# A second MLP's rows transposed two to three steps further down, and one slot's last products taken by halves

## The chip, the cores and the metric

The kernel runs on one core of a Trainium2 chip. The metric is the device time of one execution in microseconds. Besides, one execution was recorded by the hardware profiler; all rows below come from it. Engines: PE is TensorE, DVE is VectorE, ACT is ScalarE, POOL is GpSimd, SP is the engine that mostly issues DMAs (its queue is SPq, that of ScalarE ACTq).

## The reference

Three stages run one after the other.

```python
# 1 attention of 2 x 8 heads, 768 rows, head size 64; a pair counts only if both fall in one hash bucket
scores = np.where(q_bucket[:, :, :, None] == k_bucket[:, :, None, :], scale * q @ k.T, -1e9)
x = softmax(scores) @ v                               # -> 1536 tokens x 512
# 2 a mixture of 8 experts, one per token (512 -> 1024 -> 512)
e_idx = argmax(x @ w_gate + modality_bias[modality_id])
x2[e_idx == e] = gate_w * (relu(x[e_idx == e] @ w1[e]) @ w2[e])
# 3 a second, dense MLP (512 -> 2048 -> 512) on all 1536 tokens
h = x2 @ w_in
out = (maximum(h, 0) + log1p(exp(-abs(h)))) @ w_out
```

All is in float32. A product of the experts or of the MLP is made of three: each operand is split in a high and a low part, and high x high, high x low and low x high are summed.

## The kernel before, in words

**Experts.** The tokens are sorted by expert into slots of 128. Slots 0 to 16 always run; four more stand under a branch that this input doesn't take. `pipe` writes the slots out as a pipeline: the first layer of slot s (`g1`, four chunks c), its `relu`, its transposes (`hT`), and between them the second layer of slot s-1 (`g2`). `split` turns one raw weight chunk into its high part (ACT, L995) and its low part (DVE, L1000). `yout` scales a slot's result and scatters its rows with an indirect DMA (POOL, L1128) into `x2_dram`, in sorted order, with the token's number in column 513. The profile prints `x2_dram` as `x_dram`, and the tile `x2` of the second MLP as `x`.

**Second MLP.** The sorted rows are 12 tiles j of 128, in three groups g of four tiles. `x2load(j)` loads a tile into one of two buffers (`x2_p`, `bufs=2`). `x2prep(j)` transposes it on PE (`ps_x`, four 128x128 transposes, L1252), makes the high part on ACT (`x2H`, L1254) and the low part on DVE (`x2L`, L1255), and copies column 513 to `oidx` (L1258, on DVE for j = 4 and 5, else on POOL). Tile j+2 goes into the buffer of tile j, so its load waits until all readers of tile j are done, the copy to `oidx` included.

`mlp()` runs steps n over `seq`, in which four blocks f of 128 hidden units are taken for g = 0, then for g = 1, then for g = 2. Step n issues `mlp1(g, f)` (12 products into `ps_f`, three ACT passes `ga`, on DVE `gg`, then `gH` and `gL`) and then `mlp2` of the step before (12 products into `ps_o`). In steps 1, 2, 5 and 9 the DVE also converts a weight block (`wconv`, three passes that make `w` from the loaded `wraw`), and `wsplit` makes `mwH` (ACT) and `mwL` (DVE) of a block converted before. `wload` loads the next block on SP's queue. Step 0's `mlp1` is issued earlier, among the experts.

Each engine works through its own instructions in the order in which this code issues them. Group 1 is first used in step 4, group 2 in step 8. Loads of tiles 0 to 3 are issued by ACT, those of 4 to 11 by SP.

Of the kernel before, what the change touches and what calls it, by code (L numbers as in the profile page):

```python
# [16 lines left out]
P = 128  # L17
# [462 lines left out]
class Moe:  # L480
# [651 lines left out]
    def pipe(self, a, b, hook):  # L1132

        if a > 1:
            self.order(a, b)
            for _ in range(3):
                self.split()
            self.xT(a)
        for s in range(a, b + 1):
            if a + 2 <= s + 2 < b and s > 1:  # L1140
                self.gather(s + 2)
            if s < b:
                for c in range(4):
                    self.g1(s, c)

                    if s > a or c != 2:
                        self.split()
                    elif s + 1 < b:
                        self.xT(s + 1)
                self.relu(s)  # L1150
                self.reload()
            hook(s, 0)
            for c in range(4):
                if s > a:
                    self.g2(s - 1, c)
                    self.split()
                if s < b and c in (1, 2):
                    self.hT(s, c - 1)
                    if s == a and c == 2:
                        self.split()  # L1160
                if a < s < b - 1 and c == 0:
                    self.xT(s + 1)
            self.reload()
            hook(s, 1)
            if s > a:
                self.yout(s - 1)
# [68 lines left out]
    def x2load(self, j):  # L1235
        t = self.x2_p.tile([P, self.D + 1], F32, tag="x2", name="x2")

        r = (j + 2) % self.TT * P
        (self.nc.scalar if j < 4 else self.nc.sync).dma_start(out=t, in_=self.x2_dram[r:r + P, :])
        self.x2[j] = t  # L1240

    def x2prep(self, j):
# [108 lines left out]
    def mlp(self):  # L1351

        NF, CH, pend = self.NF, self.CH, self.pend
        NG = self.TT // 4
        seq = [(g, c * CH + k) for c in range(NF // CH) for g in range(NG) for k in range(CH)]
        self.late.update(seq[-CH:])

        for f in range(CH, NF):
            c, k = divmod(f, CH)
            at = (c - 1) * NG * CH + (1, 2, 5, 9)[k]  # L1360
            conv, then = self.step.get(seq[at], ((), []))
            self.step[seq[at]] = (f, then + [(self.wsplit, CH - 1)] * (f == CH))
            self.step[seq[at + 1]] = ((), [(self.wsplit, f)] + [(self.wload, f + 2)] * (f + 2 < NF))
        for n, (g, f) in enumerate(seq):

            j = 4 + 2 * {0: 0, 2: 1, 3: 2, 5: 3}.get(n, NF)
            if j < self.TT:
                if n:
                    self.x2prep(j - 2)
                    self.x2prep(j - 1)  # L1370
                self.x2load(j)
                self.x2load(j + 1)
            elif n == 6:
                self.x2prep(self.TT - 2)
                self.x2prep(self.TT - 1)
            if n == len(seq) - CH:
                self.sA.close()
                self.x2b = self.sA.enter_context(self.tc.tile_pool(name="late", bufs=1, reuse_waits="tile"))
            if n:
                pend.append((g, f) + self.mlp1(g, f))  # L1380
            if len(pend) > 1 and pend[0][:2] not in self.late:
                self.mlp2(*pend.pop(0))

        last = [(i, x) for i in range(4) for x in pend]
        n = len(pend)
        last[n - 1:n + 1] = last[n:n + 1] + last[n - 1:n]
        for i, x in last:
            self.mlp2(*x, tiles=[i])
# [245 lines left out]
```

## Time and profile before

| | |
|---|---|
| time, median of 3 runs | 771.82 us (771.51 to 772.5) |
| the profiled execution: time | 769.36 us |
| the profiled execution: span from first to last instruction | 767.6 us |
| PE busy | 748.5 us, 98% of the span |
| DVE, ACT, POOL busy | 596.5, 522.3, 227.9 us |
| mean granted clock of TensorE | 0.996 |

A busy PE means that a product was in flight; the products of the MLP follow each other every 0.23 us though each lasts 0.39 us. Idle time of another engine costs nothing by itself.

### The profile page before, as it was taken

The page shows a single profiled execution, that of the slowest core. Times are in us where ns is not written, and L with a number is a line of the kernel's source. Part 1 is how long each engine was busy: PE and PEld are TensorE (multiplying, and loading weights), DVE is VectorE, ACT ScalarE, POOL GpSimd, SP SyncE. Part 2 cuts the span into 40 slices and gives each one's busy share as a digit, 9 for nine tenths or more (in the row PEclk, how much of TensorE's full clock was granted, in tenths as well). Part 3 has the DMA queues.
Part 4 walks back from the last instruction along what each step waited for, and adds up shares of the span by engine and source line. Part 5 has one row for each costly group of instructions (what it writes and reads, how often), then busy time and mean ns, then how long its engine had stood idle before and what let it go on. Part 6 is the DMA issues. An engine that isn't in the chain of part 4 may idle for free.

```text
span 767.6 us, 13126 instructions
## 1 busy us (share of the span) xinstructions
PE 748.5 (98%) x4232; PEld 646.6 (84%) x4232; DVE 596.5 (78%) x894; ACT 522.3 (68%) x872; POOL 227.9 (30%) x608
## 2 busy tenths in 40 slices
PE   8999999999999999999999999899999999999995
PEld 6899999999999867888888888688888888888874
DVE  6898888989888889999999999765557557564442
ACT  5787887877879758899898999464544344433330
POOL 4554544446565567322312132200000000000222
PEclk9999999999999999999999999999999999999999
DMA  8845637536480014679973642351111113000111
GB/s 197 192 122 132 166 73 165 149 93 166 144 243 30 2 49 133 219 242 358 362 269 116 206 153 83 101 183 65 56 54 59 53 55 110 1 0 1 55 56 55
DMA packets 72602, 95.29 MB, mean 124 GB/s; under 512 B 31842, under 2 KB 48226, under 8 KB 72528
## 3 DMA queue, kind: packets, MB, share of 16 engines
q1 hardware_dynamic: 67152, 83.85, 36.6%
q0 software_dynamic: 3744, 9.45, 3.5%
q10 hardware_dynamic: 1632, 1.08, 0.5%
q8 instruction: 35, 0.57, 0.3%
q14 instruction: 39, 0.32, 0.1%
HBM read 105.18 MB, written 10.76 MB: 151 GB/s over the span
## 4 chain that ended last, share of the span: by engine, by line
PE 91%; POOL 2%; DVE 2%; issue 2%; DMA 1%; ACT 1%; POOLq 0%; ACTq 0%; SPq 0%; DVEq 0%
PE ps_f L1302 17%; PE ps_o L1335 17%; PE ps_y L1116 11%; PE ps_g L1069 10%; PE ps_o L310 9%; PE s L253 9%; PE ps_t L286 8%; PE s L332 2%; PE ps_prep L184 2%; PE ps_ht L1087 2%; PE ps_prep L178 2%; PE ps_xt L1042 1%; PE ps_x L1252 1%; DMA x<-x_dram 1%; POOL xg L987 1%
## 5 line engine op out<-in xcount | busy, mean ns | idle before, releaser
L1000 DVE TENSOR_TENSOR wL<-wr,wH 128x1024 fp32r<-128x1024 f32 (+1 forms) x137 | 161.3, 1207 | 9.0 <-ACT wH L995 8.9
L995 ACT CAST wH<-wr 128x1024 fp32r<-128x1024 f32 (+1 forms) x144 | 141.4, 1005 | 8.7 <-PE ps_g L1069 3.6
L1304 ACT ACTIVATE ga<-ps_f 128x512 f32<-128x512 f32 x48 | 28.7, 599 | 128.8 <-PE ps_f L1302 125.2
L263 DVE TENSOR_REDUCE mx<-s 128x1 f32<-128x768 f32 x96 | 91.5, 954 | 20.7 <-PE s L332 17.3
L274 ACT ACTIVATE p<-s,nb,sc 128x768 f32<-128x768 f32 x96 | 95.9, 999 | 15.9 <-POOL nb L265 13.1
L1310 DVE SCALAR_TENSOR_TENSOR gg<-ps_f,ga 128x512 f32<-128x512 f32 x48 | 33.2, 692 | 94.0 <-ACT ga L1306 92.0
L296 DVE TENSOR_TENSOR PL<-ps_t,PH 128x512 fp32r<-128x512 f32 x144 | 98.3, 683 | 6.8 <-ACT PH L291 6.4
L291 ACT CAST PH<-ps_t 128x512 fp32r<-128x512 f32 x144 | 83.7, 587 | 15.1 <-PE ps_t L286 12.6
L253 PE MATMUL s<-K,Q 76*128 76x384 f32 (+1 forms) x384 | 88.4, 351 | 2.6 <-ACT K L239 0.9
L310 PE MATMUL ps_o<-PH,vhl 128*128 128x256 f32 x288 | 86.8, 317 | 0.4 <-ACT Os L316 0.4
L286 PE MATMUL ps_t<-ident,p 128*128 128x128 f32 x576 | 86.3, 272 | 0.6 <-DVE PL L296 0.6
L1344 POOL DMA_INDIRECT out_dram<-acc,oidx x12 | 11.7, 972 | 231.0 <-DVE acc L1342 227.9
L1302 PE MATMUL ps_f<-x2H,mwH 128*128 128x512 f32 x192 | 76.1, 396 | 0.7 <-PEq L1206 0.7
L1335 PE MATMUL ps_o<-mwH,gH 128*128 128x512 f32 x192 | 75.5, 393 | 0.4 <-DVE gH L1317 0.4
L1335 PE MATMUL ps_o<-mwL,gH 128*128 128x512 f32 x192 | 75.8, 395 | 0.0
L1302 PE MATMUL ps_f<-x2H,mwL 128*128 128x512 f32 x192 | 75.6, 394 | 0.0
L1302 PE MATMUL ps_f<-x2L,mwH 128*128 128x512 f32 x192 | 75.6, 394 | 0.0
L1335 PE MATMUL ps_o<-mwH,gL 128*128 128x512 f32 x192 | 75.6, 394 | 0.0
L286 PEld LDWEIGHTS ps_t<-ident,p 128*128 128x128 f32 x576 | 69.4, 141 | 2.5 <-PE s L253 0.9
L310 PE MATMUL ps_o<-PL,vhl 128*64 128x256 f32 x288 | 68.3, 280 | 0.0
L253 PEld LDWEIGHTS s<-K,Q 76*128 76x128 f32 (+1 forms) x384 | 63.2, 189 | 4.3 <-ACT p L274 1.7
L1128 POOL DMA_INDIRECT x_dram<-y,cpi x17 | 19.0, 1118 | 125.9 <-ACT y L1123 89.6
(293 smaller groups left out, 1654.5 us busy)
## 6 DMA issues: line engine op xcount, KB each, us to landing
wr<-in_moe_w_dram SPq DMA_DIRECT2D x136, 512.0 KB
wraw<-in_moe_w_in_dram SPq DMA_DIRECT2D x16, 512.0 KB
wraw<-in_moe_w_out_dram SPq DMA_DIRECT2D x16, 512.0 KB
Q<-qH SPq DMA_DIRECT2D x28, 192.0 KB
K<-kH SPq DMA_DIRECT2D x28, 192.0 KB
rawv<-in_v_dram SPq DMA_DIRECT2D x8, 384.0 KB
x_dram<-x SPq DMA_DIRECT2D x8, 384.0 KB
rawq<-in_q_dram SPq DMA_DIRECT2D x14, 192.0 KB
```

What stands on the lines that cost most here:

```text
L253: self.nc.tensor.matmul(s[:, h, :HS], d[l, j][:kk, ts], d[r, j][:kk, h * HS:(h + 1) * HS], start=(a == 0), stop=(a == 1))
L263: nc.vector.tensor_reduce(mx, s[:, :, :self.HS], axis=AX.XY, op=ALU.max)
L274: self.nc.scalar.activation(e["P"][ti].rearrange("p (h c) -> p h c", h=2), s[:, :, :self.HS], AF.Exp, scale=sc, bias=nb, accum_out=e["sum" ...
L286: self.nc.tensor.transpose(ps[:, kk, t], e["P"][t][:, kt * P:(kt + 1) * P], self.ident)
L291: self.nc.scalar.copy(e["PH"][:, 2 * bk:2 * bk + 2].rearrange("p k n -> p (k n)"), e["T", bk])
L296: self.nc.vector.tensor_tensor(e["PL"][:, sl].rearrange("p k n -> p (k n)"), e["T", bk], e["PH"][:, sl].rearrange("p k n -> p (k n)").bitc ...
L310: self.nc.tensor.matmul(O[:n, :2 * P], vh[:, j, kt, :n], e[nm][:, kt], start=(kt == 0 and n == P), stop=(kt == NT - 1 and n == P))
L995: self.nc.scalar.copy(self.wt[s, c][0][:, sl], self.raw[c][:, sl])
L1000: eng.tensor_tensor(L[:, sl], self.raw[c][:, sl], H[:, sl].bitcast(F32), op=ALU.subtract)
L1116: nc.tensor.matmul(ps, a[:, f], ww[:, w], start=(f == 0 and n == 0), stop=(f == self.KF - 1 and n == 2))
L1302: nc.tensor.matmul(ps, w[:, 0, sl], x[:, k], start=(k == 0 and n == 0), stop=(k == self.KD - 1 and n == 2))
L1335: nc.tensor.matmul(self.ops[i], a[:, sl], w[:, 1], start=(k == 0 and n == 0), stop=(k == self.CH - 1 and n == 2))
```

## The change

Three edits.

1. In `mlp()` the calls of `x2prep` and `x2load` move. Tiles 4 and 5 are transposed ahead of `mlp1` of step 3 (before: step 2), tiles 6 and 7 behind `mlp1` of step 3 (before: ahead of it), tiles 8 and 9 behind `mlp1` of step 5 (before: ahead of it), tiles 10 and 11 behind `mlp1` of step 7 (before: ahead of that of step 6). The loads of tiles 6 to 11 move along, each pair behind the transposes that free its buffers.
2. The loads of tiles 4 to 7 are issued by ACT instead of SP.
3. In the slot that a pipeline starts with (slot 1), the last chunk's six products are ordered by halves of the output: three for the first 512 columns, then three for the second.

```diff
             if s < b:
                 for c in range(4):
-                    self.g1(s, c)
+
+                    self.g1(s, c, (0, 1) if s == a and c == 3 else None)
...
-        (self.nc.scalar if j < 4 else self.nc.sync).dma_start(out=t, in_=self.x2_dram[r:r + P, :])
+        (self.nc.scalar if j < 8 else self.nc.sync).dma_start(out=t, in_=self.x2_dram[r:r + P, :])
...
+        def rows(js):
+            for x, j in zip((self.x2prep, self.x2load), js or ()):
+                if j:
+                    x(j)
+                    x(j + 1)
         for n, (g, f) in enumerate(seq):
 
-            j = 4 + 2 * {0: 0, 2: 1, 3: 2, 5: 3}.get(n, NF)
-            if j < self.TT:
-                if n:
-                    self.x2prep(j - 2)
-                    self.x2prep(j - 1)
-                self.x2load(j)
-                self.x2load(j + 1)
-            elif n == 6:
-                self.x2prep(self.TT - 2)
-                self.x2prep(self.TT - 1)
+            rows({0: (None, 4), 3: (4, 6)}.get(n))
...
             if n:
                 pend.append((g, f) + self.mlp1(g, f))
+            rows({3: (6, 8), 5: (8, 10), 7: (10, None)}.get(n))
             if len(pend) > 1 and pend[0][:2] not in self.late:
                 self.mlp2(*pend.pop(0))
```

On VectorE, from the low part of weight block 3 (`mwL_8081`) on, before (tile 4 is `x_8049`, tile 5 `x_8051`; `mwL_8151` is block 4):

```order
L1291 TENSOR_TENSOR mwL_8081<-w_8030,mwH_8080 128x1024
L1255 TENSOR_TENSOR x2L<-ps_x_8102,x2H 128x4x128
L1258 CAST oidx<-x_8049 128x1
L1255 TENSOR_TENSOR x2L<-ps_x_8111,x2H 128x4x128
L1258 CAST oidx<-x_8051 128x1
L1310 SCALAR_TENSOR_TENSOR gg<-ps_f,ga 128x512
L1276 TENSOR_SCALAR w_8145<-wraw 128x1024
L1319 TENSOR_TENSOR gL<-gg,gH 128x512
L1278 SCALAR_TENSOR_TENSOR w_8145<-wraw,w_8145 128x1024
L1280 SCALAR_TENSOR_TENSOR w_8145<-wraw,w_8145 128x1024
L1291 TENSOR_TENSOR mwL_8151<-w_8075,mwH_8150 128x1024
```

And the same stretch of VectorE now:

```order
L1292 TENSOR_TENSOR mwL_8081<-w_8030,mwH_8080 128x1024
L1311 SCALAR_TENSOR_TENSOR gg<-ps_f,ga 128x512
L1277 TENSOR_SCALAR w_8122<-wraw 128x1024
L1320 TENSOR_TENSOR gL<-gg,gH 128x512
L1279 SCALAR_TENSOR_TENSOR w_8122<-wraw,w_8122 128x1024
L1281 SCALAR_TENSOR_TENSOR w_8122<-wraw,w_8122 128x1024
L1292 TENSOR_TENSOR mwL_8128<-w_8075,mwH_8127 128x1024
L1256 TENSOR_TENSOR x2L<-ps_x_8148,x2H 128x4x128
L1259 CAST oidx<-x_8049 128x1
L1256 TENSOR_TENSOR x2L<-ps_x_8157,x2H 128x4x128
L1259 CAST oidx<-x_8051 128x1
```

The work on tiles 4 and 5 went behind all of step 2's DVE work. On ScalarE, from the end of the experts (the branch) on, the rows before are these (`mwH_8080` is block 3):

```order
L1206 UNCONDITIONAL_BRANCH x2
L1304 ACTIVATE ga<-ps_f 128x512
L1305 ACTIVATE ga<-ga 128x512
L1306 ACTIVATE ga<-ga 128x512
L1315 CAST gH<-gg 128x512
L1290 CAST mwH_8080<-w_8030 128x1024
```

Now two DMA issues, the loads of tiles 4 and 5, stand ahead of step 1's passes:

```order
L1207 UNCONDITIONAL_BRANCH x2
L1240 DMA x_8049<-x_dram 128x513
L1240 DMA x_8051<-x_dram 128x513
L1305 ACTIVATE ga<-ps_f 128x512
L1306 ACTIVATE ga<-ga 128x512
L1307 ACTIVATE ga<-ga 128x512
```

The loads came from SP's queue, where nothing but weight loads stood behind them. On PE the transposes of tiles 6 and 7 (`x_8165`, `x_8167`) now stand between the first-layer products of step 3 and the second-layer products of step 2:

```order
L1303 MATMUL ps_f<-x2H,mwL_8081 128x512
L1253 MATMUL ps_x_8199<-ident,x_8165 128x128 x4
L1253 MATMUL ps_x_8207<-ident,x_8167 128x128 x4
L1336 MATMUL ps_o<-mwH_7425,gH 128x512
```

Everything that PE issues behind them is the same as before, but for the pairs 8 and 9 and 10 and 11, which moved in the same way.

## Rows read from the trace of the kernel before

**Rows 1.** The waits, PE: line, releaser, us in total, times, longest.
```profile
PE ps_x L1252 <- DMA x<-x_dram: 2.9, 1, 2.9
...
PE ps_ht L1087 <- ACT h L1077: 0.9, 1, 0.9
```

**Rows 2.** The chain that ended last, 484 to 500: start, length, what.
```profile
488.73 3.40 DMA x_dram<-y,cpi
...
492.20 4.21 DMA x<-x_dram
```

**Rows 3.** The timeline, PE, second MLP: start, length, then the instruction.
```profile
493.21 0.39 PE L1335 MATMUL ps_o<-mwH,gL 128*128 128x512 f32 x1
...
503.15 1.03 PE L1252 MATMUL ps_x<-ident,x 128*128 128x128 f32 x8
503.94 0.48 PE L1302 MATMUL ps_f<-x2H,mwH 128*128 128x512 f32 x1
...
506.82 0.39 PE L1335 MATMUL ps_o<-mwH,gH 128*128 128x512 f32 x1
...
509.77 0.40 PE L1302 MATMUL ps_f<-x2L,mwH 128*128 128x512 f32 x1
...
533.82 0.40 PE L1302 MATMUL ps_f<-x2L,mwH 128*128 128x512 f32 x1
```

**Rows 4.** The timeline, SP's queue, second MLP.
```profile
490.12 0.39 SPq L1265 DMA_DIRECT2D wraw<-in_moe_w_in_dram  x1
...
492.20 0.82 SPq L1239 DMA_DIRECT2D x<-x_dram  x2
...
499.86 0.32 SPq L1239 DMA_DIRECT2D x<-x_dram  x1
...
503.82 0.85 SPq L1239 DMA_DIRECT2D x<-x_dram  x2
```

**Rows 5.** The timeline, ACT, second MLP.
```profile
490.91 0.60 ACT L1304 ACTIVATE ga<-ps_f 128x512 f32<-128x512 f32 x1 [2.93 <-PE ps_f L1302]
```

**Rows 6.** The timeline, DVE, second MLP.
```profile
492.87 0.69 DVE L1310 SCALAR_TENSOR_TENSOR gg<-ps_f,ga 128x512 f32<-128x512 f32 x1 [2.78 <-ACT ga L1306]
...
498.39 0.68 DVE L1255 TENSOR_TENSOR x2L<-ps_x,x2H 128x512 fp32r<-128x512 f32 x1
...
502.54 0.69 DVE L1310 SCALAR_TENSOR_TENSOR gg<-ps_f,ga 128x512 f32<-128x512 f32 x1 [2.75 <-ACT ga L1306]
...
508.06 1.28 DVE L1255 TENSOR_TENSOR x2L<-ps_x,x2H 128x512 fp32r<-128x512 f32 x2
509.26 0.68 DVE L1310 SCALAR_TENSOR_TENSOR gg<-ps_f,ga 128x512 f32<-128x512 f32 x1
...
511.57 1.22 DVE L1291 TENSOR_TENSOR mwL<-w,mwH 128x1024 fp32r<-128x1024 f32 x1 [0.26 <-ACT mwH L1290]
...
534.30 0.69 DVE L1319 TENSOR_TENSOR gL<-gg,gH 128x512 fp32r<-128x512 f32 x1
```

**Rows 7.** The timeline, POOL, second MLP.
```profile
502.66 0.18 POOL L1258 CAST oidx<-x 128x1 int32<-128x1 f32 x1 [0.61 <-DMA x<-x_dram]
...
510.39 0.18 POOL L1258 CAST oidx<-x 128x1 int32<-128x1 f32 x1 [0.50 <-DMA x<-x_dram]
```

**Rows 8.** Busy times by stretch: length, engines, then PE's granted clock, DMA share, GB/s.
```profile
10.00:12.00 2.00, 0.64 (x2) 0.19 (x1) 1.91 (x5) 1.24 (x3) 1.84 (x5) 1.00 0.98 212
14.00:16.00 2.00, 2.00 (x11) 2.00 (x10) 1.87 (x4) 1.06 (x3) 1.25 (x5) 0.50 1.05 269
16.00:18.00 2.00, 2.00 (x10) 2.00 (x9) 1.04 (x3) 2.00 (x4) 1.15 (x3) 0.69 0.78 203
494.00:496.00 2.00, 0.00 (x0) 0.00 (x0) 1.91 (x3) 1.16 (x2) 0.00 (x0) 1.00 0.97 360
```

**Rows 9.** The timeline, ACT, the end of slot 1's first layer.
```profile
287.86 1.05 ACT L995 CAST wH<-wr 128x1024 fp32r<-128x1024 f32 x1
288.81 1.09 ACT L1077 ACTIVATE h<-ps_g 128x512 f32<-128x512 f32 x2
```

## The prediction

> **What bounds the kernel now.** I read the waits of PE first. PE is the engine on which the chain of waits ends nearly everywhere, so only its idle time can be won, and only new idle time on it can be lost. Two of its waits lie where the change works: 2.9 us for the load of tile 4, and 0.9 us for slot 1's `h` [rows 1]. Then the chain around the first: the last slot's scatter lands at 492.13, SP issues the loads of tiles 4 and 5 at 492.20, tile 4 is there 4.21 us later [rows 2], while PE has issued its last product of `mlp2(0)` at 493.21 [rows 3]. Then the timeline of each engine behind that, because the change moves work on all of them. The reader is to see there that PE runs without a gap from 496.55 on, and that DVE is nearly as full: step 1's work takes it from 492.87 to 498.39, step 2's from 502.54 to 508.06, 5.52 us each [rows 6], with no idle time shown inside either.
>
> All starts are in the profiled execution, 769.36 us long, which is 2.46 us under the median; I add the difference to the median of 771.82.
>
> **The removed wait.** Without the transposes of tiles 4 and 5 in step 2, PE goes on at 493.45 (493.21 plus the pitch of 0.23) with `mlp1` of step 2, which needs only group 0. By itself that is worth up to 2.9 us. The question is what is late next.
>
> **ACT is held at the scatter.** The two load issues now stand on ACT ahead of step 1's `ga`. They need the landing at 492.13, just as SP's did, so they go out at 492.20 and take 0.82 us [rows 4]. ACT is free at 493.02 instead of starting `ga` at 490.91 [rows 5]. From `ga` to `gg` it is 492.87 - 490.91 = 1.96 us [rows 5, 6], so `gg` of step 1 starts at 494.98, 2.11 later. No row of before shows an ACT issue that waits, so the bounds are 0 (ACT passes it by) and 2.1 us (ACT stands). I take 2.1, because ACT's instructions start in program order wherever I looked in the timeline. The Trainium skill speaks against this edit too: "TensorE: Matmul & The Clock Gate", section on the 16 sub-arrays, says that ScalarE and VectorE take their queue strictly first in, first out, and only PE reorders a little. By that the forecast stands as given below; if a waiting issue were passed by, the time would be some 2.1 us less.
>
> **Tiles 6 and 7 come late: the main term.** Their loads go into the buffers of 4 and 5 and cannot go out before `oidx` of 4 and 5 has been copied on DVE. In the order now, that copy stands behind all DVE work of steps 1 and 2. Step 2's work is ready when DVE comes to it: ACT is through with `gH` and `mwH` at most 2.31 us behind a `gg` (509.26 to 511.57, where `mwL` had to wait for `mwH`), and `ga` takes 1.96 more, which makes 499.3, while DVE is through with step 1 at 500.5 [rows 6]. So the low part of tile 4 starts 2 x 5.52 = 11.04 us behind `gg`, at 506.02 [rows 6]. In the trace of before, tile 7's load went out at 499.86, 1.47 us after tile 4's low part had started at 498.39 [rows 4, 6]. Now that is 507.49, issued by ACT, which holds step 3's `ga` meanwhile.
>
> How long that load takes: 2.80 us when hardly anything else moved (499.86 to 502.66), 6.1 at the other end (the second issue of the pair at 503.82, some 0.49 later, to 510.39) [rows 4, 7]. I take 4.3. The nearest case is tile 4's own load, which took 4.21 with a weight block issued 2.08 us ahead of it [rows 2, 4]. Here the load of block 7 goes out on SP as soon as DVE has converted block 5, about 1.8 us ahead of tile 6's load. So tile 7 is there at 511.8, its transposes start 0.14 later, as tile 4's did, and take half of 0.79 us [rows 3]; `mlp2` of step 2 starts at 512.3.
>
> PE stands before these transposes from about 503.1. Up to that point it has 2.8 us for `mlp1(2)`, 0.4 waiting for step 1's late `gH` and `gL`, 2.8 for `mlp2(1)`, 0.8 for the transposes of 4 and 5, 2.9 for `mlp1(3)`, counted from 493.45. It then stands idle for some 8 us. Before, `mlp2` of step 2 started at 506.82 with exactly the same work behind it [rows 3]. The loss here, with the removed wait already counted in, is 512.3 - 506.8 = **5.5 us**.
>
> With the load's other values it is 4.0 and 7.3. The lower end is cut off by a second chain. ACT is free at 507.9, `gg` of step 3 follows at 509.9, `mwL` of block 5 2.31 us later, then 1.22 for it and 1.28 for the low parts of tiles 6 and 7 [rows 6]: 514.7. The second product of step 4 needs these and stood at 509.77 [rows 3]. So the range is 4.9 to 7.3.
>
> **Tiles 10 and 11 come late for step 8.** They are now transposed behind `mlp1` of step 7, with only `mlp2` of step 6 between them and their first use. Their low parts stand on DVE behind `gL` of step 7. That `gL` started at 534.30; it comes 0.79 earlier against the rest, since the pair's transposes no longer stand ahead of it. So the low parts are done at 534.30 - 0.79 + 0.69 + 1.28 = 535.5 [rows 3, 6], and the second product of step 8, which needs all of them, stood at 533.82 [rows 3]: **1.6 us** of new waiting (1.0 to 1.7). PE is without gaps behind it, so nothing gives it back. Tiles 8 and 9 have a whole step more and cost nothing.
>
> **The clock.** After the long idle time PE's granted clock may fall. In the trace it was at 0.50, that is 1.2 of 2.4 GHz, over all of 14 to 16 us and still 0.69 on average from 16 to 18, shortly after a stretch in which PE was busy for 0.64 of 2 us; after the 2.9 us of waiting at 493.6 it stayed at 1.00 [rows 8]. An idle time of 8 us is far over both, so I expect a fall. About 3.3 us at half speed (2 from the one stretch, 1.24 from the other) lose **1.7 us**. The ends are 0, as after 493.6, and 3.4, if it stays low twice as long. The Trainium skill, same page, section on what is actually happening, holds the slow state to be the normal one, which activity lifts; the trace agrees, and by it the 1.7 belong in the sum; without them it would come out at 779.
>
> **Slot 1 by halves.** The aim must be the 0.9 us in front of `hT` [rows 1]. But ACT starts `relu` at 288.81, without idle time, straight behind a weight cast that began at 287.86 [rows 9]. The first half could be ready earlier and ACT would still not take it. I take 0; the bounds are -0.9, the whole wait, and +0.2, should the low weight part be late for the second product.
>
> **Sum:** 5.5 + 1.6 + 1.7 + 0 = 8.8 us. 769.36 + 8.8 = 778.2 for the profiled execution, 771.82 + 8.8 = **780.6 us** for the median.
>
> **Rivals.**
> - *The clock stays up* after the idle time: 771.8 + 7.1 = 778.9. The 2.9 us at 493.6 speak for it, the fall at 14 us against. Chance 0.15.
> - *ACT is not held at the scatter:* all of the DVE chain comes 2.1 earlier, and with it tile 7: 780.6 - 2.1 = 778.5. Against it, the order of ACT. Chance 0.1.
> - *The loads of 6 and 7 take about 6 us* beside the weight block: 780.6 + 1.8 = 782.4. Chance 0.1.
> - *Not slower:* tile 7 is loaded behind `mlp1(3)`, because its issue waits only for the transposes of 4 and 5 and not for DVE. PE then runs through from 493.45 and `mlp2` of step 2 starts at 503.9, 2.9 us early; less the 1.6 at step 8, 770.5. It decides from where load 7 goes out: by 500.3, it is there when PE is done at 503.1 (with 2.80 us). For it: before, tile 7 was there at 502.66, half a microsecond ahead of its use [rows 3, 7]. Against it: SP's issue at 499.86 came only after tile 4's low part at 498.39 and what follows it on DVE, long after the transposes of 496.55. Chance 0.05.
> - The forecast itself: 0.6.
>
> **Numbers.** A difference under 0.2%, 1.5 us, can't be told from no change. The not slower case lies just within it or a little under, so faster 0.02, same 0.04, slower 0.94. For the range I take the lower rivals together at the bottom, ACT not held and the clock up, 771.8 + 5.0 = 776.8, and a little below; at the top slow loads with a somewhat longer low clock, 783.5. 776.5 to 783.5 leaves about 0.15 outside.
>
> **What would show it.** In the trace of the changed kernel: `ga` of step 1 starts some 2 us later on ACT, behind two ACTq issues at about 492.2; DVE works from `gg` of step 1 to `oidx` of tile 5 without a gap; PE waits some 8 us for the load of tile 6 or 7 with all of `mlp1(3)` behind it; the granted clock is 0.50 in a stretch right there; the second product of step 8 waits 1.6 us for `x2L`; and the wait for `h` in slot 1 is still about 0.9. If the two loads go out before DVE has reached tile 4, the main term is wrong; if PE's wait there is under 3 us, the sign may be.

## The result: 7.5 us slower

Over four runs each, the changed kernel takes a median of 779.21 us (778.27 to 779.97) and the kernel before 771.66 (771.13 to 772.5). The ratio is 1.0102, with an interval of 1.0086 to 1.0118. The profiled execution of the changed kernel took 779.03 us, with a span of 777.3. (The transposes moved by half a step to one and a half steps, as the list of the change has it, and not by two to three, as the title says.)

Before any start time is compared, one shift has to be taken out. ACT's last `y` of the MoE starts at 488.39 in this execution, and 487.29 in the profiled execution of before; the scatter behind it lands 1.10 us later. Other executions with the same code up to there have it at 487.34 or 488.44, so this is no work of the change. In this section, differences that hang on the scatter are less 1.10.

PE's waits over the whole span (line, releaser, us in total, times, longest):

```profile
PE ps_x L1253 <- DMA x<-x_dram: 8.1, 1, 8.1
PE ps_f L1303 <- DVE x2L L1256: 1.4, 1, 1.4
...
PE ps_ht L1087 <- ACT h L1077: 0.8, 1, 0.8
```

The 2.9 us for tile 4 [rows 1] are gone. In their place stand 8.1 us for tile 6 and 1.4 us for low parts in step 8. Slot 1's wait for `h` is as it was. The next three views show how the 8.1 come about. First ACT's timeline in the second MLP (start, length, instruction, idle time before it and what ended it):

```profile
488.39 0.69 ACT L1123 ACTIVATE y<-ps_y,gsl 128x512 f32<-128x512 f32 x1 [2.67 <-issue]
493.25 0.81 ACTq L1240 DMA_DIRECT2D x<-x_dram  x2
494.11 0.60 ACT L1305 ACTIVATE ga<-ps_f 128x512 f32<-128x512 f32 x1 [5.04 <-DMA x_dram<-y,cpi]
...
507.88 0.98 ACTq L1240 DMA_DIRECT2D x<-x_dram  x2
508.91 0.60 ACT L1305 ACTIVATE ga<-ps_f 128x512 f32<-128x512 f32 x1 [4.06 <-DVE oidx L1259]
```

Twice a `ga` stands right behind two DMA issues and is released by what the *issue* waited for: once by the landing of the scatter, once by `oidx` on DVE. `ga` of step 1 moved from 490.91 [rows 5] to 494.11, which is 2.1 us less the shift. DVE's timeline has what follows from it:

```profile
496.07 0.69 DVE L1311 SCALAR_TENSOR_TENSOR gg<-ps_f,ga 128x512 f32<-128x512 f32 x1 [4.89 <-ACT ga L1307]
...
501.59 0.69 DVE L1311 SCALAR_TENSOR_TENSOR gg<-ps_f,ga 128x512 f32<-128x512 f32 x1
...
504.82 1.23 DVE L1281 SCALAR_TENSOR_TENSOR w<-wraw,w 128x1024 int32<-128x1024 int32 x1
505.96 1.22 DVE L1292 TENSOR_TENSOR mwL<-w,mwH 128x1024 fp32r<-128x1024 f32 x1
507.10 0.68 DVE L1256 TENSOR_TENSOR x2L<-ps_x,x2H 128x512 fp32r<-128x512 f32 x1
507.70 0.14 DVE L1259 CAST oidx<-x 128x1 int32<-128x1 f32 x1
```

From the first `gg` to tile 4's low part it is 11.03 us, without an idle time between. The last three rows show who is served in which order: a conversion and a split of a weight block, then tile 4's low part, then the copy for which the load of tile 6 waits. The load itself takes 4.52 us (the chain that ended last: start, length, what):

```profile
507.88 4.52 DMA x<-x_dram
```

PE's timeline around it, and in step 8:

```profile
500.62 1.04 PE L1253 MATMUL ps_x<-ident,x 128*128 128x128 f32 x8
...
504.06 0.40 PE L1303 MATMUL ps_f<-x2H,mwL 128*128 128x512 f32 x1
512.53 1.94 PE L1253 MATMUL ps_x<-ident,x 128*128 128x128 f32 x8 [8.08 <-DMA x<-x_dram]
514.12 0.78 PE L1336 MATMUL ps_o<-mwH,gH 128*128 128x512 f32 x1
...
517.79 0.40 PE L1303 MATMUL ps_f<-x2L,mwH 128*128 128x512 f32 x1
...
543.38 0.50 PE L1303 MATMUL ps_f<-x2L,mwH 128*128 128x512 f32 x1 [1.41 <-DVE x2L L1256]
```

`mlp2` of step 2 starts at 514.12, against 506.82 [rows 3]: 6.2 us later. The products of `mlp2` themselves take no longer: 0.39 to 0.40 us each from 515.49 on, as before. Those at 512.53 and 514.12 are, and the busy times by stretch say why (length, PE, PEld, DVE, ACT, POOL, PE's granted clock, DMA share, GB/s):

```profile
506.00:508.00 2.00, 0.00 (x0) 0.00 (x0) 2.00 (x5) 0.00 (x0) 0.00 (x0) 1.00 0.33 46
508.00:510.00 2.00, 0.00 (x0) 0.00 (x0) 0.50 (x2) 1.06 (x2) 0.00 (x0) 0.64 1.00 360
...
512.00:514.00 2.00, 1.47 (x7) 1.50 (x8) 1.51 (x2) 1.49 (x3) 0.70 (x2) 0.50 0.06 21
514.00:516.00 2.00, 2.00 (x9) 1.68 (x8) 1.70 (x3) 0.83 (x2) 0.00 (x0) 0.66 0.62 158
```

The clock fell to 0.50 (1.2 GHz) at about 508.6, in the middle of the idle time, and came back at about 515.4. PE had work only from 512.53 on, so 2.8 us of work ran at half speed and lost 1.4.

### The profile page after: what moved, and what is told of

It reads as the page before. It is cut to its first block, busy times and chain, and to the rows that moved or that the text cites. A ratio compares the mean times of both kernels' runs of the same rounds, so it can differ in the third digit from the quotient of the medians.

```text
span 777.3 us, 13129 instructions
## 1 busy us (share of the span) xinstructions
PE 751.1 (97%) x4231; PEld 647.3 (83%) x4232; DVE 596.4 (77%) x894; ACT 522.0 (67%) x872; POOL 232.8 (30%) x608
## 4 chain that ended last, share of the span: by engine, by line
PE 88%; DVE 3%; POOL 2%; issue 2%; DMA 2%; ACT 1%; POOLq 0%; ACTq 0%; DVEq 0%
PE ps_f L1303 16%; PE ps_o L1336 16%; PE ps_y L1116 11%; PE ps_g L1069 10%; PE ps_o L310 9%; PE s L253 8%; PE ps_t L286 8%; PE s L332 2%; PE ps_prep L184 2%; PE ps_ht L1087 2%; PE ps_prep L178 1%; PE ps_xt L1042 1%; PE ps_x L1253 1%; DMA x<-x_dram 1%; POOL xg L987 0%
## 5 line engine op out<-in xcount | busy, mean ns | idle before, releaser
L1128 POOL DMA_INDIRECT x_dram<-y,cpi x17 | 22.3, 1312 | 123.2 <-ACT y L1123 88.9
```

## The experiments

All were timed against runs of the kernel before on the same chip. "+" and "-" are against that median.

**What the two loads on ACT cost.** The changed kernel, with the loads of tiles 4 to 7 back on SP.

```
-        (self.nc.scalar if j < 8 else self.nc.sync).dma_start(out=t, in_=self.x2_dram[r:r + P, :])
+        (self.nc.scalar if j < 4 else self.nc.sync).dma_start(out=t, in_=self.x2_dram[r:r + P, :])
```

> The changed kernel with the loads of tiles 4 to 7 back on SP's queue. Theory (ACT stands at the scatter and holds all of VectorE's work behind it): step 1's ga starts 2 us earlier, tile 7's load goes out about 2 us earlier and, with no weight block just ahead of it, takes about 3 us; some 3 us faster than the changed kernel, about +4.7 us against before (+3.3 if the clock stays up). Rival (which engine issues the loads doesn't matter, the copy of oidx alone decides): within 0.5 us of the changed kernel.

Measured: 775.19, +3.8, ratio 1.0048 [1.0031, 1.0064]. `ga` of step 1 is free of the scatter. The loads of 6 and 7 leave 3.4 us earlier, of which 0.9 is the scatter's earlier landing in this execution, and tile 6 is there 2.76 us after its issue, with no weight block just ahead of it. PE still waits for tile 6:

```profile
490.60 0.60 ACT L1305 ACTIVATE ga<-ps_f 128x512 f32<-128x512 f32 x1 [2.41 <-PE ps_f L1303]
```
```profile
504.44 0.98 SPq L1240 DMA_DIRECT2D x<-x_dram  x2
```
```profile
507.34 1.94 PE L1253 MATMUL ps_x<-ident,x 128*128 128x128 f32 x8 [4.80 <-DMA x<-x_dram]
```

So by the medians some 3.8 of the 7.5 us are due to the choice of ACT. The trace shows that the saving was larger and that the clock took part of it back. It fell at about 506.4 and came back at about 513.2, with PE at work for nearly all of that time:

```profile
506.00:508.00 2.00, 0.66 (x3) 0.69 (x4) 1.44 (x2) 1.22 (x2) 0.74 (x1) 0.59 0.91 294
508.00:510.00 2.00, 2.00 (x9) 1.79 (x9) 1.23 (x3) 1.17 (x2) 0.64 (x2) 0.50 0.99 311
510.00:512.00 2.00, 2.00 (x6) 1.58 (x5) 0.62 (x1) 0.00 (x0) 0.00 (x0) 0.50 0.98 344
512.00:514.00 2.00, 2.00 (x8) 1.57 (x7) 0.00 (x0) 0.00 (x0) 0.18 (x1) 0.70 0.13 49
```

That lost 2.8 us, twice as much as in the changed kernel; the table near the end has it beside the others.

**What the copy on DVE costs.** The changed kernel, with `oidx` of tiles 4 and 5 copied on POOL, as of all others.

```
-        (nc.vector if g == 1 and i < 2 else nc.gpsimd).tensor_copy(self.oidx[g][:, i:i + 1], x[:, self.D:])
+        nc.gpsimd.tensor_copy(self.oidx[g][:, i:i + 1], x[:, self.D:])
```

> The changed kernel with the oidx copies of tiles 4 and 5 on GpSimd instead of VectorE, loads still on ACT. Theory (the loads of tiles 6 and 7 wait for that copy behind two steps of VectorE work): the loads go out behind the high parts on ACT, some 3.5 us earlier; PE's wait for them falls from 8.1 to about 3.5 to 4 us; then VectorE's low parts of tiles 6 and 7 bind, which leaves about +3.8 us against before. Rival (the load itself or the transfers beside it make the wait): the wait stays over 7 us and the time within 1 us of the changed kernel.

Measured: 773.8, +2.4 where +3.8 was expected, ratio 1.0034 [1.0021, 1.0048]. The loads left at 501.50 instead of 507.88, and still PE waited:

```profile
501.50 0.81 ACTq L1240 DMA_DIRECT2D x<-x_dram  x2
```
```profile
506.20 1.28 DVE L1256 TENSOR_TENSOR x2L<-ps_x,x2H 128x512 fp32r<-128x512 f32 x2
```
```profile
506.94 1.25 PE L1253 MATMUL ps_x<-ident,x 128*128 128x128 f32 x8 [3.38 <-DVE x2L L1256]
```

This releaser was in no account so far: the expectation had the low parts of tiles 6 and 7 as the next bound, and this is that of tile 4. Transposes go to one of two PSUM buffers, and tile 6 needs the one that tile 4's low part on DVE still reads; that low part started at 506.20. So a load that comes in time would not have been enough. DVE holds PE back in two ways, the copy and the PSUM buffer, and the first one is only the longer. The clock fell behind this wait too (0.58 and 0.57 in 508 to 512), which cost 1.6 us.

**What tiles 8 to 11 cost.** The changed kernel, with their transposes back ahead of steps 5 and 6.

```
-            rows({0: (None, 4), 3: (4, 6)}.get(n))
+            rows({0: (None, 4), 3: (4, 6), 5: (8, 10), 6: (10, None)}.get(n))
...
-            rows({3: (6, 8), 5: (8, 10), 7: (10, None)}.get(n))
+            rows({3: (6, 8)}.get(n))
```

> The changed kernel with tiles 8 to 11 back where they were (ahead of steps 5 and 6). Theory: the 1.4 us that PE waits for low parts in step 8 is gone and nothing else changes, so 1.4 us faster than the changed kernel, about +6.1 against before. Rival (that wait is slack which a later one takes up): the same time as the changed kernel.

Measured: 777.19, +5.8, ratio 1.008 [1.0057, 1.0103]. The wait in step 8 is gone, the one for tile 6 stays at 7.9 us. The time is some 1.8 us less than the changed kernel's. That fits the wait in step 8, which put back the products behind it by 1.7 us: step 8's first product starts 7.99 us later than before, those behind the wait 9.66.

**What the halves in slot 1 do.** The kernel before, with this edit alone.

```
-                    self.g1(s, c)
+                    self.g1(s, c, (0, 1) if s == a and c == 3 else None)
```

> The kernel before with the third edit alone (slot 1's last products by halves). Theory (ACT takes the relu only behind its weight cast, so an earlier half wins nothing): 0 us against before, within 0.3, and PE still waits 0.8 to 0.9 us for h in slot 1. Rival (the wait for h is the products' order): 0.9 us faster, and that wait gone.

Measured: 771.21, -0.2, ratio 1.0 [0.9985, 1.0015]. The `relu` still starts straight behind a weight cast on ACT, and PE waits 0.9 us for it, as before [rows 1, 9]:

```profile
288.61 1.05 ACT L995 CAST wH<-wr 128x1024 fp32r<-128x1024 f32 x1
289.56 1.09 ACT L1077 ACTIVATE h<-ps_g 128x512 f32<-128x512 f32 x2
```

**The loads of 4 to 7 on ACT alone**, in the kernel before.

```
-        (self.nc.scalar if j < 4 else self.nc.sync).dma_start(out=t, in_=self.x2_dram[r:r + P, :])
+        (self.nc.scalar if j < 8 else self.nc.sync).dma_start(out=t, in_=self.x2_dram[r:r + P, :])
```

> The kernel before with the second edit alone: loads of tiles 4 to 7 on ACT. Theory (ACT stands at the scatter and then at the copy of oidx): step 1's gg starts 2.1 us later, all of VectorE's work behind it too, tile 7's load goes out 2.1 us later beside a weight block, and PE, which had that load half a microsecond before it was needed, waits 2 to 3 us for it: 1.5 to 3 us slower than the median of before. Rival (PE waits for tile 4 anyway, which hides it): 0 us.

Measured: 772.43, +0.7, ratio 1.0016 [1.0004, 1.0028]; a miss, less than expected. `ga` was held as said (494.16, again behind 5.04 us of idle time that ended with the scatter), and the loads of 6 and 7 left only at 502.41. But their transposes started at 506.94 without a wait. In the order of before they stand behind `mlp1` of step 2 and `mlp2` of step 1, and in this execution the clock was at 0.50 to 0.72 from 496 to 504, behind the wait for tile 4, so PE itself came late:

```profile
496.00:498.00 2.00, 0.32 (x2) 0.35 (x3) 1.80 (x3) 1.24 (x3) 0.00 (x0) 0.72 0.59 216
...
502.00:504.00 2.00, 2.00 (x7) 1.57 (x6) 1.03 (x4) 0.00 (x0) 0.00 (x0) 0.57 0.96 308
```
```profile
497.68 1.94 PE L1252 MATMUL ps_x<-ident,x 128*128 128x128 f32 x8 [3.41 <-DMA x<-x_dram]
...
506.94 1.03 PE L1252 MATMUL ps_x<-ident,x 128*128 128x128 f32 x8
```
```profile
506.61 0.18 POOL L1258 CAST oidx<-x 128x1 int32<-128x1 f32 x1 [15.73 <-DMA x<-x_dram]
```

From the transposes of tile 4 to those of tile 6 it is 9.26 us here and 6.60 in the profiled execution of before (496.55 to 503.15). At that pace, an estimate, PE would have stood at tile 6 at 504.3, some 2.3 us ahead of its load. So the wait of the theory may well be there when the clock stays up; this execution can't show it. By the medians, the same hold that costs 3.8 us in the changed order costs 0.7 in the old one.

**Is the clock a cost of the change?** Three runs. First the changed kernel with 30 products that nobody uses ahead of the transposes of 6 and 7:

```
+            if n == 3:
+                H, _ = self.mw[0]
+                ps = self.py.tile([P, 512], F32, tag="py", name="ps_busy")
+                for _ in range(30):
+                    self.nc.tensor.matmul(ps, H[:, 0, :P], self.x2t[0][0][:, 0], start=True, stop=True)
```

> The changed kernel with 30 idle-filling products (7 us, their result is used by nothing) on PE just ahead of the transposes of tiles 6 and 7, to keep the granted clock up in the wait; about 1 us of the wait stays. Theory (the fall of the clock costs 1.4 us behind the wait): clock 1.00 throughout, 1.4 us faster than the changed kernel, that is about 777.8. Rival (the clock's cost is hidden behind VectorE's low parts): the same time as the changed kernel, 779.2.

Measured: 777.01, ratio 1.0072 [1.0056, 1.0088]. The clock stays up. The transposes start behind 0.94 us of idle time after the last filler, released by the same load:

```profile
508.00:510.00 2.00, 2.00 (x11) 1.63 (x10) 0.00 (x0) 1.78 (x3) 0.00 (x0) 1.00 1.05 398
510.00:512.00 2.00, 1.06 (x7) 0.52 (x5) 1.20 (x2) 1.25 (x3) 0.18 (x1) 1.00 0.60 229
512.00:514.00 2.00, 2.00 (x12) 1.68 (x12) 1.74 (x3) 1.38 (x3) 0.22 (x1) 1.00 0.35 76
```

Then the kernel before with 10 such products ahead of the transposes of 4 and 5 (the same code, at step 2):

> The kernel before with 10 idle-filling products (2.3 us) on PE ahead of the transposes of tiles 4 and 5, inside its wait for tile 4. Theory (in most runs of the kernel before the clock falls behind this wait too, and the profiled execution of 769.36 is one where it didn't): some 1.5 us faster than before, 769.5 to 770, with less spread than 769.2 to 774. Rival (the clock stays up in before): 0 us.

Measured: 769.86 (769.15 to 770.61), -1.4, ratio 0.9978 [0.9968, 0.9987], while the kernel before ran from 770.04 to 773.85 beside it. The clock is at 1.00 from 494 to 502. Last, the kernel before itself once more, with a profile:

> The kernel before, unchanged, profiled once more. Theory: PE waits 3 to 3.5 us for tile 4 as before, and the granted clock falls to 0.50 behind it in most executions, which then take 771 us or more; in one in which it stays at 1.00 the time is about 769.5. Rival (the clock never falls there): clock 1.00 from 490 to 510 and still 771.

Measured: 771.12. PE's wait for tile 4, and the busy times by stretch:

```profile
496.71 1.24 PE L1252 MATMUL ps_x<-ident,x 128*128 128x128 f32 x8 [3.37 <-DMA x<-x_dram]
```
```profile
496.00:498.00 2.00, 1.29 (x9) 1.13 (x10) 2.00 (x2) 0.56 (x2) 0.00 (x0) 0.96 0.07 27
498.00:500.00 2.00, 2.00 (x6) 1.52 (x6) 1.50 (x5) 0.57 (x2) 0.00 (x0) 0.50 0.04 4
500.00:502.00 2.00, 2.00 (x8) 1.58 (x7) 0.00 (x0) 0.00 (x0) 0.18 (x1) 0.69 0.90 273
```

In this execution of the *old* kernel the clock fell at about 497.8, behind a wait of 3.4 us for tile 4, and was back at about 501.2. From the transposes of tile 4 to `mlp2` of step 2 PE took 11.81 us (496.71 to 508.52) where it took 10.27 in the profiled execution of the prediction (769.36, wait 2.9, clock at 1.00). So the fall cost 1.5 us, most of the distance of 1.8 between the two executions. The old kernel seems to pay for such a fall in many of its runs: of the 62 beside the experiments, the 22 with a mean granted clock of 0.996 or more have a median of 770.35 us, and the 39 with 0.994 or less one of 771.75. The new one pays for a fall elsewhere. With the clock held up in both, they are 777.01 - 769.86 = 7.15 us apart.

**What would have made the new order work.** Three runs, from the changed kernel, all with tiles 8 to 11 where they stood before. The first has four row buffers and loads tiles 4 to 7 on SP at the start, so that neither ACT nor the copy is in the way:

```
-        t = self.x2_p.tile([P, self.D + 1], F32, tag="x2", name="x2")
+        t = self.x2_p.tile([P, self.D + 1], F32, tag="x2", name="x2", bufs=4)
...
-        (self.nc.scalar if j < 8 else self.nc.sync).dma_start(out=t, in_=self.x2_dram[r:r + P, :])
+        (self.nc.scalar if j < 4 else self.nc.sync).dma_start(out=t, in_=self.x2_dram[r:r + P, :])
...
-            rows({0: (None, 4), 3: (4, 6)}.get(n))
+            if n == 0:
+                for j in range(4, 8):
+                    self.x2load(j)
+            rows({3: (4, 8), 5: (8, None), 6: (10, None)}.get(n))
...
-            rows({3: (6, 8), 5: (8, 10), 7: (10, None)}.get(n))
+            rows({3: (6, 10)}.get(n))
```

> The changed kernel with four row buffers instead of two, the loads of tiles 4 to 7 all on SP at the start of the stage, and tiles 8 to 11 transposed where they were before. No load waits for a copy now. Theory (behind the copy, VectorE itself is the bound: the transposes of 6 and 7 need the buffers in PSUM that 4 and 5 free by their low parts, and step 4 needs the low parts of 6 and 7): PE still waits about 0.5 us ahead of tile 6 and 1.4 us in step 4, so the gain is lost again down to about -2 us against the median of before, of which most is the clock that stays up. Rival (only the late load cost time): both waits under 0.3 us and -3.5 us or more.

Measured: 770.24, -1.0, ratio 0.9984 [0.9975, 0.9993]; half of what was expected. The two waits are 1.9 and 1.0 us, where 0.5 and 1.4 were expected. PE's waits from 480 to 560:

```profile
PE ps_x L1253 <- DVE oidx L1259: 1.9, 1, 1.9
PE ps_f L1303 <- DVE x2L L1256: 1.0, 1, 1.0
```

Both are on DVE, where tile 4's low part still started only at 504.52, straight behind a split of a weight block:

```profile
503.39 1.22 DVE L1292 TENSOR_TENSOR mwL<-w,mwH 128x1024 fp32r<-128x1024 f32 x1
504.52 0.68 DVE L1256 TENSOR_TENSOR x2L<-ps_x,x2H 128x512 fp32r<-128x512 f32 x1
```

The second leaves loads, copy and buffers as the change has them and moves that weight work instead: the conversions of blocks 4 to 7 from steps 1, 2, 5 and 9 to 4, 6, 8 and 10.

```
+        self.step[seq[1]] = ((), [(self.wsplit, CH - 1)])
...
-            at = (c - 1) * NG * CH + (1, 2, 5, 9)[k]
+            at = (c - 1) * NG * CH + ((4, 6, 8, 10) if c == 1 else (1, 2, 5, 9))[k]
...
-            self.step[seq[at]] = (f, then + [(self.wsplit, CH - 1)] * (f == CH))
+            self.step[seq[at]] = (f, then)
```

> The changed kernel (loads on ACT, copy on VectorE, two buffers) with tiles 8 to 11 where they were before, and the conversions of weight blocks 4 to 7 moved from steps 1, 2, 5, 9 to 4, 6, 8, 10. Theory (two conversions and two splits ahead of the copy make the loads of 6 and 7 late): without them the load of tile 7 goes out near 502.7 instead of 507.5, PE waits about 2 us there, the clock stays up; 768.5 to 769.5. Rival (the two issues on ACT make the delay): over 5 us of waiting stay and the time is over 774.

Measured: 768.98 (768.79 to 769.06), -2.3, ratio 0.9964 [0.9951, 0.9978]. On DVE tile 4's low part follows `gL` at once, the copy is made at 501.99, and the loads leave 0.18 later; PE waits 1.5 us for them, and the clock stays at 1.00:

```profile
500.78 0.69 DVE L1320 TENSOR_TENSOR gL<-gg,gH 128x512 fp32r<-128x512 f32 x1
501.39 0.68 DVE L1256 TENSOR_TENSOR x2L<-ps_x,x2H 128x512 fp32r<-128x512 f32 x1
501.99 0.14 DVE L1259 CAST oidx<-x 128x1 int32<-128x1 f32 x1
```

The changed kernel with only tiles 8 to 11 back was at +5.8, so moving the weight work is worth some 8 us. Against the old kernel with fillers, whose clock stays up (769.86 on the same chip), this version is only 0.9 us faster.

The third puts the two together, and issues tile 6's and 7's high parts on ACT ahead of step 3's `ga`:

```
-    def mlp1(self, g, f):
+    def mlp1(self, g, f, mid=None):
...
+        if mid:
+            mid()
         a = self.gp.tile([P, 512], F32, tag="ga", name="ga")
...
-                pend.append((g, f) + self.mlp1(g, f))
-            rows({3: (6, 8), 5: (8, 10), 7: (10, None)}.get(n))
+                pend.append((g, f) + self.mlp1(g, f, (lambda: rows((6, 10))) if n == 3 else None))
```

> A version built from the findings: four row buffers with the loads of tiles 4 to 7 on SP at the start of the stage, the conversions of weight blocks 4 to 7 in steps 4, 6, 8, 10, the high parts of tiles 6 and 7 ahead of step 3's passes on ACT, tiles 8 to 11 where they were before. Theory: no wait over 0.5 us is left on PE between the branch and step 8, the clock stays up, and the 3 us that PE waited for tile 4 are won: 766.5 to 767.3. Rival (another bound stands right behind, ACT or the transfers, as it did each time so far): 768.5 or more, with a wait of over 1 us in steps 3 or 4.

Measured: 767.25 (766.61 to 767.48), -4.5, ratio 0.995 [0.9937, 0.9964]. It beats both kernels. Its profiled span, 764.9 us, is 2.7 shorter than the 767.6 of the profiled execution of before, which had no fall of the clock behind tile 4; the rest of the 4.5 us is most likely what other runs of the old kernel lose. Between 480 and 560 PE has one wait left in its list:

```profile
PE ps_f L1303 <- PEq L1207: 0.5, 1, 0.5
```

## Why the prediction held, and where it did not

**The hold on ACT: right.** 2.1 us forecast, 2.1 measured. The reason given, that ACT starts in program order, shows in the idle time of 5.04 us ahead of `ga` that ended with the scatter. The strict order that the Trainium skill states in "TensorE: Matmul & The Clock Gate", section on the 16 sub-arrays, agrees with it. Another page, "DMA: Bandwidth & Descriptors", section "Issuing engines are not separate DMA queues", says that starting DMAs from several engines at once only saves the sequencer's time for the issue, which is usually small beside the DMA. The runs here show a larger price, that of issues that have to wait: by the medians, the same loads on ACT instead of SP cost some 3.8 us.

**The DVE chain and the late load: right.** From `gg` to tile 4's low part 11.04 us were forecast and 11.03 measured; the load took 4.52 us where 4.3 were taken. `mlp2` of step 2 starts 514.12 - 506.82 - 1.10 = 6.2 us late. Of that, 0.8 belong to the clock: the transposes took 1.59 us up to the next product (512.53 to 514.12) and 0.79 before [rows 3]. The 5.4 left answer to the 5.5 of the sum.

**What I missed in it:** the second way by which DVE holds PE, the PSUM buffer. It did not change the number, since the load came later. But the rival "not slower" supposed that an early load alone lets PE run through. The run with the copy on POOL had the early load, and PE waited 3.4 us. That rival could not have come true, for a reason that I had not seen.

**Step 8: right.** 1.6 us forecast. The idle time is 1.41 us, and the products behind it are put back by 1.7.

**Slot 1: right.** Nothing, since ACT and not PE's products sets the start of `relu`.

**The clock: right in the trace, wrong in the sum.** It fell as said, and cost 1.4 us where 1.7 were forecast. The failed step is that I added the whole of it to a median. The profiled execution of before was one without a fall behind the wait for tile 4, while another, at 771.12, shows one that cost 1.5. The 2.46 us between profile and median, which I carried over as a constant, most likely held a fall already; the runs behind that median have no trace to show it. So the median forecast seems to have counted most of it twice: 780.6 - 1.7 = 778.9 against 779.21 measured. It is by chance the number of the rival "the clock stays up", which the trace refutes. The comparison with the clock held up on both sides gives 7.15 us, and the terms without a clock, 5.5 + 1.6, gave 7.1.

**What adds up.** The table compares profiled executions with that of before (span 767.6), by the starts of the same products of PE, in us. The clock's part is what the work from tile 6's transposes to step 4 took beyond the 3.63 us that it takes in the last version above, with the clock at 1.00 and no wait inside (in the run with the copy on POOL, less 0.2 for a wait for DVE inside it). The scatter's part is the start of the last `y`.

| execution | step 4 later | of it the clock | of it the scatter | left: tiles 6 and 7 | step 8 and behind | span longer by |
|---|---|---|---|---|---|---|
| the changed kernel | 8.0 | 1.4 | 1.1 | 5.5 | 1.7 | 9.7 |
| tiles 8 to 11 back | 7.7 | 2.1 | 0.2 | 5.4 | 0.0 | 7.7 |
| 30 fillers | 5.8 | 0.0 | 0.3 | 5.4 | 1.6 | 7.4 |
| loads on SP | 4.2 | 2.8 | 0.2 | 1.2 | 1.7 | 5.9 |
| copy on POOL | 2.8 | 1.6 | 0.2 | 1.0 | 1.7 | 4.5 |

The sums close to 0.1 us. The main term of 5.5 us shows in three executions, whatever the clock did. Taking away either the hold on ACT or the copy on DVE brings it down to about 1 us, so their prices can't be added. The changed kernel with fillers gained 2.2 us by the medians where 1.4 were expected; between the two profiled executions 0.8 of 2.3 us is the earlier scatter. What makes the scatter land earlier or later stays open: in the changed kernel's execution 0.7 of the 1.1 us is there at the first slot's `y` already.

## What to carry over

When a step is moved down an order, look at everything that its *release* feeds, and at the queue in which that release then stands: here a copy of one column on DVE, behind weight work that nobody needed for many steps, kept a load, ACT and PE waiting. Moving that weight work turned the same idea, with tiles 8 to 11 left where they were, from 5.8 us slower to 2.3 us faster. And before a clock fall is added to a median, check with a second profile whether the runs behind that median do not contain one already.

## What the runs showed of the hardware

- Two DMA issues on ACT that had to wait held the compute behind them: ACT was idle ahead of `ga` for 5.04 us at the scatter and for 4.06 us at the copy.
- A wait of 2.9 us on PE left the granted clock at 1.00, and waits of 3.4 us in other executions in the old order were followed by a fall. This is one reason why runs of the old kernel lie 3.8 us apart on the chip where those with fillers in the wait lie within 1.5; runs at the same mean clock still differ by over 3.
- The low time was not always the same: 3.4 us behind the wait of 3.4 us in the old kernel, 6.8 us behind a wait as long with its loads on ACT, and 6.8 in the changed kernel. Only the work inside it pays: 2.8 of the 6.8 us in the changed kernel, which lost 1.4, and nearly all of it with the loads back on SP, which lost 2.8.
- Products that nobody uses, in a wait, were worth 1.4 us in the old kernel.
